# Weights rounded beside a spectrum: one piece begun at a time, and a later change of load buffers

## The chip, the cores and the metric

The kernel runs on one core of a Trainium2 chip. The metric is the time of one execution on the device in microseconds (us), the median of three runs. The engines are named as in the profile: PE is TensorE's matmul stream and PEld its weight loads, DVE is VectorE, ACT is ScalarE, POOL is GpSimd, SP is SyncE, whose queue (SPq) issues every transfer of this kernel.

## What is computed

Two batches of 3008 positions with 256 features pass a spectral layer and then two MLPs. The spectral layer takes a real FFT along the positions, mixes the features with a complex 256 x 256 matrix, adds a bias, pulls real and imaginary part towards zero by 0.01 and goes back:

```python
X = np.fft.rfft(x, axis=1)
Yr = Xr @ w_r - Xi @ w_i + b_r
Yi = Xr @ w_i + Xi @ w_r + b_i
Yr = np.sign(Yr) * np.maximum(np.abs(Yr) - 0.01, 0.0)
Yi = np.sign(Yi) * np.maximum(np.abs(Yi) - 0.01, 0.0)
y = np.fft.irfft(Yr + 1j * Yi, n=3008, axis=1)
h = y.reshape(6016, 256) @ w_in            # 256 x 2048
y = (h / (1 + np.exp(-h))) @ w_out         # 2048 x 256
h = y @ w_in2
out = np.maximum(0.01 * h, h) @ w_out2
```

All matmuls work on pairs of reduced-precision numbers: each float32 operand is split into a high and a low part (names ending in hi and lo, or h and l), and three products are summed. The weights are float64 in memory (two 32-bit words each) and have to be rounded to float32 on the chip before they are split.

## The kernel before

**Stages.** First comes a DFT over 47 points (L255, to about 47 us). Then 48 *items* (`items`, a frequency group k and a batch b) go through the spectrum. `spectrum(j)` (L366) runs eight stages, each on an item of another age (`STAGES`, L364): threshold (L334), split_a (L297), split_z (L316), split_y (L341) and store (L357) on ACT and DVE, then on PE mix (L307, tile pz), forward (L325, py) and backward (L349, pb). store copies pb to one of three buffers bo on ACT (L360) and sends it to memory, scr (L361). For the first 28 items one matrix dm serves two items; from item 28 on each item loads and splits its own (dmr, L213; dmh on ACT, L222; dml on POOL, L223). Then an inverse transform reads scr back (bt, L381; matmuls px, L408; splits xhi and xlo, L415 and L416), and the MLPs run over chunks of 512 positions, in steps f of 128 hidden features (ph, L505; acc, L575). The last items of the spectrum run between the first MLP steps.

**The weights beside it.** `weight_pieces` (L98) cuts w_in and w_out of the first MLP into 32 pieces of 128 x 256 numbers, 256 KB each; they are counted from 0 here. A piece passes five steps: `load` (L112) takes a buffer wraw and issues the transfer on SP; `begin` (L119) makes a rounded candidate on ACT (L123, L125) and DVE (L128, L130); `scale` (L133) reads wraw for the last time (DVE, L135); `around` (L139) adds on POOL (L142); `split` (L145) makes the two parts on ACT (L149) and POOL (L150). Each step hands the piece to the next by a list: loaded, begun, scaled, rounded, made.

Three drivers call them. `step` (L153) does a full round, during the DFT and in MLP steps f from 3 on (`between`). `third` (L169) is called after each item j of the loop at L386, with j % 3: at 0 it splits a piece and begins one, at 1 it scales the oldest begun piece, at 2 it adds and loads. `until` runs rounds until enough pieces are made.

**Buffers and order.** `raws` is a list of pools; `load` takes from the first. Up to item 32 that is the pool early with three buffers wraw, which lives in memory that the MLPs take over later; after `raws.pop(0)` it is the pool stage, with two (L115). Each engine works in the order in which the program names its instructions, and SP issues its transfers in that order too: a transfer whose buffer is still in use waits at the head of the queue.

Of the kernel before, what the change touches and what calls it, by code (L numbers as in the profile page):

```python
# [71 lines left out]
def spectral_mlp_kernel(ctx, tc, x, w_r, w_i, b_r, b_i, w_in1, w_out1, w_in2, w_out2, da, ea, dm, out):  # L72
# [23 lines left out]
    def weight_pieces(win, wout, in_dst, out_dst):  # L96

        win, wout = win.bitcast(U32), wout.bitcast(U32)
        pieces = []
        for q in range(NF // 2 + 1):
            if q < NF // 2:
                for d in range(2):
                    pieces.append((win[d * 128:(d + 1) * 128, q * 512:(q + 1) * 512], [w[:, d * DFF + q * 256:d * DFF + (q + 1) * 256] for w in in_dst]))
            if q:
                for f in (2 * q - 2, 2 * q - 1):
                    pieces.append((wout[f * 128:(f + 1) * 128, :], [w[:, f * D:(f + 1) * D] for w in out_dst]))
        loaded, begun, scaled, rounded, made = [], [], [], [], []  # L110

        def load():  # L112
            if pieces:
                src, dst = pieces.pop(0)
                raw = raws[0].tile([128, 512], F32, tag="wraw", name="wraw", bufs=3 if raws[1:] else 2).bitcast(U32)  # L115
                nc.sync.dma_start(out=raw, in_=src)
                loaded.append((raw.rearrange("p (e w) -> p e w", w=2), dst))

        def begin():  # L119
            raw, dst = loaded.pop(0)  # L120
            m = stage.tile([128, 256], U32, tag="wm", name="wm", bufs=2)
            c = stage.tile([128, 256], F32, tag="wc", name="wc", bufs=4).bitcast(U32)
            nc.scalar.activation(out=c, in_=raw[:, :, 0], func=ACTF.Copy, scale=2.0 ** -29)  # L123

            nc.scalar.activation(out=m.bitcast(F32), in_=raw[:, :, 1].bitcast(F32), func=ACTF.Copy, scale=2.0 ** -112)  # L125
            yield

            nc.vector.tensor_scalar(out=m.bitcast(F32), in0=m.bitcast(F32), scalar1=MAG, scalar2=-MAG, op0=ALU.min, op1=ALU.max)  # L128
            yield
            nc.vector.tensor_scalar(out=m, in0=m, scalar1=3, scalar2=0x7FFFFFFF, op0=ALU.logical_shift_left, op1=ALU.bitwise_and)  # L130
            begun.append((raw, m, c, dst))

        def scale():  # L133
            raw, m, c, dst = begun.pop(0)
            nc.vector.scalar_tensor_tensor(out=m, in0=raw[:, :, 1], scalar=0x80000000, in1=m, op0=ALU.bitwise_and, op1=ALU.bitwise_or)  # L135
            yield
            scaled.append((m, c, dst))

        def around(add):  # L139
            m, c, dst = scaled.pop(0)  # L140
            r = dst[0].bitcast(U32) if len(dst) == 1 else c
            add.tensor_tensor(out=r, in0=c, in1=m, op=ALU.add)  # L142
            rounded.append((c.bitcast(F32), dst))

        def split():  # L145
            c, dst = rounded.pop(0)
            if len(dst) == 2:
                hi, lo = dst
                nc.scalar.copy(hi, c)  # L149
                nc.gpsimd.tensor_tensor(out=lo, in0=c, in1=hi.bitcast(F32), op=ALU.subtract)  # L150
            made.append(1)

        def step(add=nc.gpsimd):  # L153

            if scaled:
                around(add)
            parts = [p() for p, ready in ((scale, begun), (begin, loaded and len(begun) < 2)) if ready]
            done = len(rounded)
            while parts:
                for p in list(parts):  # L160
                    if next(p, parts) is parts:
                        parts.remove(p)
            for _ in range(done):
                split()
            if scaled:
                around(add)
            load()

        def third(i):  # L169

            if i == 0:
                if rounded:
                    split()
                if loaded and len(begun) < 2:
                    list(begin())
            elif i == 1 and begun:
                list(scale())
            elif i == 2 and scaled:
                around(nc.gpsimd)
                load()  # L180

        def until(n):
            while len(made) < min(n, 2 * NF):
                step()

        return load, step, third, until

    raws, parts = [stage], ("hi", "lo")
# [177 lines left out]
    def spectrum(j):  # L366
        for part, lag in STAGES:
            if 0 <= j - lag < len(items):
                part(j - lag)
        split_dm(j + 1)  # L370
        load_dm(j + 4)
# [4 lines left out]
    def load_b():  # L376
        if groups:
            g, n = groups.pop(0)
            b, p = divmod(g, R2 // 2)
            bt = btp.tile([NJ, NG, D], F32, tag="bt", name="bt")  # L380
            nc.sync.dma_start(out=bt[:, :n], in_=scr[:, b, p:p + n, :])  # L381
            bts.append((g, n, bt))

    spectrum(-1)
    n_items = len(items)
    for j in range(n_items - 1):  # L386
        spectrum(j)
        if j == n_items - KH + KT + 6:
            load_b()
            load_b()  # L390
        if j == n_items - 16:
            raws.pop(0)
        third_w(j % 3)
    right.close()
# [370 lines left out]
```

## Time and profile before

| | |
|---|---|
| median of three runs | 1232.33 us |
| lowest, highest | 1231.36, 1234.48 us |
| profiled execution | 1230.04 us |
| its span, first to last instruction | 1228.3 us |
| PE busy in the span | 1201.3 us, 98% |
| DVE, ACT, POOL busy | 844.1, 782.0, 562.3 us |
| mean granted clock of PE | 0.996 |

The span leaves out what lies around the first and the last instruction, 1.7 us here. A busy PE is not PE at its peak, since its matmuls are pipelined; a share of busy time is an average over stages with different limits. So the profile is read stage by stage: stretches of the span with the busy time of each engine, then the timelines of the engines in the stretch where PE is not full, with the idle time before an instruction and what ended it, and the chain of waits. The granted clock is a share of 2.4 GHz; it has two levels, 1.0 and 0.5 (1.2 GHz), and a figure in between is a mean over a stretch. A release that the profile names can be wrong when an instruction waits for several things.

### The profile page before, as it was taken

To read this page: it belongs to the slowest core of one execution; us is meant where nothing else is said; L and a number is where in the kernel's file an instruction comes from. 1 tells how busy PE (TensorE), PEld (TensorE's weight loads), DVE (VectorE), ACT (ScalarE), POOL (GpSimd) and SP (SyncE) were. 2 spreads that over 40 slices of the span, in tenths; PEclk is the share of its full clock that TensorE was granted. 3 is DMA by queue.
4 is the path that set the end of the run, shared out by engine and by line. 5 is a ranking of instruction groups with operands and counts; after the bars stand their busy time and mean duration, and the time that the engine had idled before them with its cause. 6 is when DMAs were issued, how large, how long until landed. Compare 5 with 4: busy or idle time off the path is not lost.

```text
span 1228.3 us, 20097 instructions
## 1 busy us (share of the span) xinstructions
PE 1201.3 (98%) x7346; PEld 1074.2 (87%) x7346; DVE 844.1 (69%) x1533; ACT 782.0 (64%) x1614; POOL 562.3 (46%) x598
## 2 busy tenths in 40 slices
PE   8899978999999999999999999999999999999998
PEld 7788867888899999989998988988898898888898
DVE  2688855667888888888888896555555555555543
ACT  4788855566666666666666677566566566655664
POOL 0333522343445444544445484454545445554532
PEclk9999989999999999999999999999999999999999
DMA  9444443101011121111110100110111011001000
GB/s 233 126 119 126 123 124 90 39 14 48 18 54 50 40 70 48 43 41 61 38 27 26 35 31 1 35 35 1 35 36 35 1 35 35 10 26 35 31 1 31
DMA packets 35883, 61.62 MB, mean 50 GB/s; under 512 B 3908, under 2 KB 15784, under 8 KB 35784
## 3 DMA queue, kind: packets, MB, share of 16 engines
q1 hardware_dynamic: 35784, 60.33, 16.1%
q8 instruction: 58, 0.95, 0.3%
q14 instruction: 41, 0.34, 0.1%
HBM read 41.70 MB, written 18.61 MB: 49 GB/s over the span
## 4 chain that ended last, share of the span: by engine, by line
PE 91%; DMA 3%; DVE 3%; ACT 1%; issue 1%; SPq 0%; ACTq 0%; DVEq 0%
PE ph L505 42%; PE acc L575 38%; PE pz L312 5%; PE py L331 3%; PE px L408 2%; DMA wraw<-in_moe_w_in_dram 2%; PE pb L354 1%; DVE wlo L468 1%; DMA scr<-bo 1%; DMA xt<-in_x_dram 1%; PE pa L255 0%; SPq L237 0%; DVE py L339 0%; DVE lb L530 0%; DVE winlo L485 0%
## 5 line engine op out<-in xcount | busy, mean ns | idle before, releaser
L530 POOL TENSOR_TENSOR la<-u,ha 128x512 fp32r<-128x512 f32 (+1 forms) x176 | 232.6, 1322 | 246.8 <-ACT ha L568 246.0
L530 DVE TENSOR_TENSOR lb<-u,hb 128x768 fp32r<-128x768 f32 (+1 forms) x176 | 178.3, 1013 | 220.4 <-ACT hb L568 218.8
L505 PE MATMUL ph<-xlo,winhi 128*128 128x512 f32 (+1 forms) x768 | 239.2, 391 | 1.2 <-POOL xlo L431 1.2
L505 PE MATMUL ph<-xhi,winlo 128*128 128x512 f32 (+1 forms) x768 | 240.2, 394 | 0.1
L505 PE MATMUL ph<-xhi,winhi 128*128 128x512 f32 (+1 forms) x768 | 237.6, 391 | 0.0
L524 ACT ACTIVATE u<-ph 128x512 f32<-128x512 f32 (+1 forms) x192 | 113.7, 592 | 153.3 <-PE ph L505 153.2
L505 PEld LDWEIGHTS ph<-xlo,winhi 128*128 128x128 f32 x768 | 144.0, 188 | 36.3 <-POOL xlo L431 5.4
L505 PEld LDWEIGHTS ph<-xhi,winhi 128*128 128x128 f32 x768 | 143.8, 188 | 30.8
L542 POOL TENSOR_TENSOR u<-u 128x256 f32<-128x256 f32 x160 | 125.8, 786 | 65.1 <-DVE u L525 58.5
L568 ACT CAST hb<-u 128x768 fp32r<-128x768 f32 (+1 forms) x176 | 140.3, 797 | 9.4 <-DVE u L556 4.9
L575 PE MATMUL acc<-lb,whi 128*128 128x256 f32 (+1 forms) x496 | 141.1, 284 | 0.0
L575 PE MATMUL acc<-hb,whi 128*128 128x256 f32 (+1 forms) x496 | 139.6, 281 | 0.0
L575 PE MATMUL acc<-hb,wlo 128*128 128x256 f32 (+1 forms) x496 | 139.5, 281 | 0.0
L525 DVE SCALAR_TENSOR_TENSOR ph<-u,ph 128x512 f32<-128x512 f32 (+1 forms) x112 | 76.6, 684 | 77.8 <-ACT u L524 77.8
L527 ACT ACTIVATE ph<-ph 128x512 f32<-128x512 f32 (+1 forms) x96 | 55.1, 574 | 113.2 <-PE ph L505 113.2
L505 PEld LDWEIGHTS ph<-xhi,winlo 128*128 128x128 f32 x768 | 120.6, 189 | 2.8 <-ACT bo L360 0.3
L568 ACT CAST ha<-u 128x512 fp32r<-128x512 f32 (+1 forms) x176 | 109.7, 623 | 14.8 <-POOL u L542 14.8
L530 DVE TENSOR_TENSOR l<-ph,h 128x512 fp32r<-128x512 f32 (+1 forms) x176 | 117.4, 667 | 0.0
L549 DVE TENSOR_TENSOR u<-ph,u 128x512 f32<-128x512 f32 x160 | 109.3, 683 | 6.3 <-POOL u L542 6.3
L568 ACT CAST h<-ph 128x512 fp32r<-128x512 f32 (+1 forms) x176 | 102.3, 581 | 2.7 <-DVE ph L525 1.6
L575 PE MATMUL acc<-ha,whi 128*128 128x256 f32 (+1 forms) x352 | 102.1, 290 | 0.0
L575 PE MATMUL acc<-la,whi 128*128 128x256 f32 (+1 forms) x352 | 100.9, 287 | 0.0
(124 smaller groups left out, 2675.9 us busy)
## 6 DMA issues: line engine op xcount, KB each, us to landing
wraw<-in_moe_w_in_dram SPq DMA_DIRECT2D x32, 256.0 KB
wraw<-in_moe_w_out_dram SPq DMA_DIRECT2D x32, 256.0 KB
scr<-bo SPq DMA_DIRECT2D x48, 128.0 KB
scr<-x2o SPq DMA_DIRECT2D x22, 256.0 KB
x2i<-scr SPq DMA_DIRECT2D x22, 256.0 KB
out_dram<-x2o SPq DMA_DIRECT2D x22, 256.0 KB
dmr<-in_dm_dram SPq DMA_DIRECT2D x34, 160.0 KB
bt<-scr SPq DMA_DIRECT2D x14, 384.0 KB
```

The costliest lines, as they stand in the source:

```text
L312: nc.tensor.matmul(pz, lhsT=u[:, h, :], rhs=v[:, h].rearrange("p g e -> p (g e)"), start=(n == 0), stop=(n == len(terms) - 1))
L331: nc.tensor.matmul(py, lhsT=u, rhs=v, start=(n == 0), stop=(n == len(terms)))
L408: nc.tensor.matmul(px[:, s * PAIR:(s + 1) * PAIR], lhsT=bt[:, s, h * 128:(h + 1) * 128], rhs=ea_sb, start=True, stop=True, skip_group_chec ...
L505: nc.tensor.matmul(ph, lhsT=u[:, h, f * 128:(f + 1) * 128], rhs=v[:, h, :], start=(i == 0), stop=(i == len(terms) - 1))
L524: nc.scalar.activation(out=th, in_=ph, func=ACTF.Tanh)
L525: nc.vector.scalar_tensor_tensor(out=out, in0=th, scalar=1.0, in1=ph, op0=ALU.add, op1=ALU.mult)
L527: nc.scalar.activation(out=out, in_=ph, func=ACTF.Prelu, alpha=0.01)
L530: eng.tensor_tensor(out=lo, in0=src, in1=hi.bitcast(F32), op=ALU.subtract)
L542: nc.gpsimd.tensor_tensor(out=blk(1), in0=blk(0), in1=blk(2), op=ALU.subtract)
L549: nc.vector.tensor_tensor(out=v[:, 3:5], in0=b22, in1=v[:, 0:2], op=ALU.subtract)
L568: nc.scalar.copy(hi, src)
L575: nc.tensor.matmul(dst, lhsT=u, rhs=v, start=(begin and self.p == 0 and i == 0), stop=(end and self.p == NF // 2 - 1 and i == 2), skip_gro ...
```

## The change

```diff
--- before.py
+++ after.py
@@ -171,7 +171,7 @@
             if i == 0:
                 if rounded:
                     split()
-                if loaded and len(begun) < 2:
+                if loaded and not begun:
                     list(begin())
             elif i == 1 and begun:
                 list(scale())
@@ -388,7 +388,7 @@
         if j == n_items - KH + KT + 6:
             load_b()
             load_b()
-        if j == n_items - 16:
+        if j == n_items - 8:
             raws.pop(0)
         third_w(j % 3)
     right.close()
```

In `third`, a piece is begun only when no other piece has been begun and not scaled; before, a second one was let in. And the load that first takes a buffer of stage is that of item 41 (the first at or after item 40 with j % 3 == 2) and no longer that of item 32. The pools and their sizes are as they were.

What that does to the order of the instructions is shown at two places. The first is SP's queue at item 41, in one piece of the difference between the kernels: the load of piece 24 between the transfers of items 41 and 42 (wraw is the load's buffer, dmr the matrix, bo the item's result).

```order
 L361 DMA scr<-bo 4x32x256 [waits Activation_49]
 L213 DMA dmr<-in_dm_dram 128x320 [waits DMAHW7_49,DMAHW6_49,Pool_49]
-L116 DMA wraw<-in_moe_w_out_dram 128x512 [waits DVE_49]
+L116 DMA wraw<-in_moe_w_out_dram 128x512
 L361 DMA scr<-bo 4x32x256 [waits DMAHW0_49,Activation_49]
 L213 DMA dmr<-in_dm_dram 128x320 [waits DMAHW2_49,DMAHW1_49,Pool_49]
```

The rows stand where they stood; the wait for DVE is gone from this row, and in the same way from that of piece 25, three items later. The row of piece 23, at item 38, reads the same in both kernels, with a wait for DVE; but it waited for the scale step of piece 21 and now waits for that of piece 20. The loads of pieces 21 and 22, which waited for no engine, now wait for the scale steps of 18 and 19.

The second place is DVE at the first two rounds in the MLP (f = 3 and 4). In the kernel before, with wraw_2320 the buffer of piece 24 and wraw_2463 that of piece 25 (wm is the candidate; L525 and L530 belong to the MLP):

```order
L135 SCALAR_TENSOR_TENSOR wm_2508<-wraw_2320,wm_2508 128x256
L128 TENSOR_SCALAR wm_2750<-wm_2750 128x256
L130 TENSOR_SCALAR wm_2750<-wm_2750 128x256
L530 TENSOR_TENSOR la_2723<-ph_2715,ha_2722 128x512
L530 TENSOR_TENSOR lb_2725<-ph_2736,hb_2724 128x512
L525 SCALAR_TENSOR_TENSOR ph_2779<-u_2790,ph_2779 128x512
L135 SCALAR_TENSOR_TENSOR wm_2750<-wraw_2463,wm_2750 128x256
```

In the changed kernel wraw_2314 is the buffer of piece 24:

```order
L128 TENSOR_SCALAR wm_2743<-wm_2743 128x256
L130 TENSOR_SCALAR wm_2743<-wm_2743 128x256
L530 TENSOR_TENSOR la_2717<-ph_2709,ha_2716 128x512
L530 TENSOR_TENSOR lb_2719<-ph_2730,hb_2718 128x512
L525 SCALAR_TENSOR_TENSOR ph_2771<-u_2782,ph_2771 128x512
L135 SCALAR_TENSOR_TENSOR wm_2743<-wraw_2314,wm_2743 128x256
```

The first round scaled piece 24 and began 25; now it begins 24, and the scale step of 24 follows in the second round, behind the MLP's L530 and L525. The load of piece 26, which takes the buffer of 24, is issued in the first round in both kernels. All later rounds of this kind are shifted in the same way, and one more round has work to do.

## Rows read from the trace of the kernel before

**Rows 1.** Stretches: length, busy time (x instructions) of each engine, PEclk, DMA share, GB/s
```profile
47.00:131.00 84.00, 83.93 (x511) 74.83 (x512) 73.42 (x161) 73.86 (x209) 32.11 (x40) 1.00 0.37 110
...
139.63:147.82 8.19, 8.06 (x50) 6.79 (x49) 7.05 (x16) 7.33 (x22) 4.21 (x6) 1.00 0.47 140
147.82:158.62 10.80, 9.88 (x58) 8.01 (x56) 7.99 (x17) 7.48 (x22) 4.77 (x6) 1.00 0.34 99
158.62:169.82 11.20, 8.56 (x48) 6.77 (x48) 7.02 (x15) 7.50 (x21) 4.20 (x5) 1.00 0.33 102
169.82:174.28 4.46, 1.46 (x10) 1.28 (x11) 2.57 (x7) 3.89 (x11) 1.68 (x3) 0.74 0.55 186
174.28:182.40 8.12, 8.12 (x32) 7.54 (x33) 3.45 (x7) 2.44 (x6) 1.47 (x2) 0.51 0.39 117
182.40:197.50 15.10, 10.58 (x60) 8.59 (x59) 7.06 (x14) 7.19 (x18) 0.00 (x0) 1.00 0.20 60
197.50:660.00 462.50, 462.50 (x2782) 409.63 (x2781) 381.72 (x689) 293.38 (x578) 211.75 (x238) 1.00 0.14 45
```

**Rows 2.** Timeline of the SP queue, 147 to 204 us: start, length, line, transfer
```profile
147.52 0.34 SPq L213 DMA_DIRECT2D dmr<-in_dm_dram  x1
153.38 0.33 SPq L116 DMA_DIRECT2D wraw<-in_moe_w_in_dram  x1
153.82 0.54 SPq L361 DMA_DIRECT2D scr<-bo  x1
...
164.18 0.33 SPq L116 DMA_DIRECT2D wraw<-in_moe_w_out_dram  x1
...
169.74 0.82 SPq L381 DMA_DIRECT2D bt<-scr  x2
175.34 0.35 SPq L116 DMA_DIRECT2D wraw<-in_moe_w_out_dram  x1
...
199.39 4.65 SPq L116 DMA_DIRECT2D wraw<-in_moe_w_in_dram  x2
```

**Rows 3.** Timeline of DVE, 152 to 180 us, same columns, [idle before <-releaser]
```profile
152.25 1.10 DVE L135 SCALAR_TENSOR_TENSOR wm<-wraw,wm 128x256 uint32<-128x256 uint32 x1
...
174.23 1.08 DVE L135 SCALAR_TENSOR_TENSOR wm<-wraw,wm 128x256 uint32<-128x256 uint32 x1
...
179.98 0.41 DVE L346 TENSOR_TENSOR yl<-py,yh 128x256 fp32r<-128x256 f32 x1
```

**Rows 4.** Timeline of ACT, 158 to 178 us, same columns as rows 3
```profile
158.62 0.37 ACT L360 COPY bo<-pb 128x256 f32<-128x256 f32 x1 [2.46 <-DMA scr<-bo]
...
164.80 0.38 ACT L360 COPY bo<-pb 128x256 f32<-128x256 f32 x1
...
169.82 0.37 ACT L360 COPY bo<-pb 128x256 f32<-128x256 f32 x1 [2.86 <-DMA scr<-bo]
...
173.36 0.38 ACT L360 COPY bo<-pb 128x256 f32<-128x256 f32 x1
...
178.02 0.47 ACT L415 CAST xhi<-px 128x376 fp32r<-128x376 f32 x1 [1.23 <-PE px L408]
```

**Rows 5.** Chain of waits, 147 to 202 us: start, length, engine and line
```profile
147.90 0.36 PE pb L354 x3
148.26 1.40 PE pz L312 x6
149.65 0.83 PE py L331 x7
...
174.28 3.70 PE px L408 x16
...
201.87 0.87 PE px L408 x8
```

**Rows 6.** One stretch of the tail of the spectrum, same columns as rows 1
```profile
187.85:193.90 6.05, 2.02 (x9) 1.40 (x9) 2.61 (x6) 2.47 (x8) 0.00 (x0) 1.00 0.09 28
```

**Rows 7.** Timeline of ACT in the MLP's first chunk, same columns as rows 3
```profile
203.11 0.43 ACT L123 ACTIVATE wc<-wraw 128x256 uint32<-128x256 uint32 x1 [0.55 <-DMA wraw<-in_moe_w_in_dram]
```

## The prediction

> **What bounds the kernel now.** I read the stretches first [rows 1]. From 197.50 us to 660 TensorE (PE) is busy for all of its time, and so it is from 47 to 131 (83.93 of 84 us). Nothing that the change moves on other engines in those two stretches can shorten or, while PE stays fed, lengthen the run; what can be won lies between. There the spectrum runs in groups of three items, and the stretches are cut where the ACT copy of bo (L360) begins that stands just ahead of each begin step. An undisturbed group takes 8.19 us (139.63 to 147.82). The next two take 10.80 and 11.20 us, and then PE works at half of its clock, 0.51, for 8.12 us.
>
> The second view is the queue of SyncE (SP), which issues every transfer [rows 2]. After 147.52 it stands still until 153.38, then issues one weight load (L116), and everything behind that load comes out in a bunch: stores of bo, then dmr. It stands again until 164.18, and until 175.34. What it waits for is on VectorE (DVE) [rows 3]: the scale step L135 begins at 152.25 and takes 1.10 us, so it ends at 153.35, and the load goes out 0.03 later; the third begins at 174.23, ends at 175.31, and the load goes at 175.34. These are loads 23, 24 and 25 (counted from 0), the third to fifth that go to the common pool, where wraw has two buffers. Three pieces are in flight there, so load 23 wants the buffer of piece 21, whose scale step comes two items later in the program than the load.
>
> The third view is what stands behind it [rows 4]. bo has three buffers. ACT's copy at 158.62 had stood 2.46 us for a store that had not landed, the one at 169.82 2.86 us. PE needs what these copies free, and runs dry. So the bound here is the SP queue, held up by a weight load that nobody needs yet.
>
> **The change, part by part.** *Loads change over 8 items from the end.* Loads 21, 22 and 23 now go to the early pool of three buffers, where each finds a buffer whose scale step ended one item before; 24 and 25 are the first users of the two common buffers and wait for no engine. All three stalls in the loop go. What is late next is the ordinary three-item pattern of ACT and DVE, 8.19 us a group:
> - group of load 23: 10.80 - 8.19 = 2.61 us
> - group of load 24: 11.20 - 8.19 = 3.01 us
>
> Behind load 24, the first inverse product (px, L408) begins at 174.28 [rows 5]. The page blames ACT, but the copy that frees its buffer begins at 173.36 and ends at 173.74 [rows 4]; what px also needs is bt, issued at 169.74 [rows 2], so bt took at most 4.54 us. In the changed kernel the copy that now begins at 164.80 [rows 4] begins 2.61 earlier, at 162.19; its store goes at about 162.6 and bt at some 163.2; with 4.54 us it lands by 167.8. px then waits only for its copy, at 173.74 - 5.62 = 168.12. That takes away 174.28 - 173.74 = **0.54 us**, with 0.3 us in hand. Load 25 follows bt and no longer holds back the stores.
>
> *The clock.* The granted clock of 169.82 to 174.28 is 0.74 on average, and 0.51 up to 182.40 [rows 1]: it fell to the 1.2 GHz level about (1 - 0.74) x 4.46 / 0.5 = 2.3 us ahead of 174.28, at 172, and came back at 182. Ahead of the fall PE had been busy 8.56 of 11.20 us, then 1.46 of 4.46. In the changed kernel those gaps go. PE's item that starts its pz at 148.26 is through at 148.26 + 1.40 + 0.83 + 0.36 = 150.85 [rows 5]; the one ahead of px stands two groups later, so it ends at 167.2, and px starts at 168.1: a gap of about 1 us. I take the clock as staying at 1.0. Of the tail that remains one stretch, 187.85 to 193.90, has PE busy 2.02 of 6.05 us with the clock at 1.00 [rows 6]. The Trainium skill has a rule that speaks against this term (TensorE: Matmul & The Clock Gate, "A second HAM failure mode: psum-queue depth-cycling"): short idles between groups of matmuls, if frequent enough, make the clock go down and up. By it the tail could bring the clock down again, and the sum would be 6.16 instead of 8.94; the trace agrees with it at 172 and not in the tail. What is the term worth? From 174.28 to 182.40 PE ran 16 px, one pz, one py and one pb. At full clock these take 2 x 0.87 + 1.40 + 0.83 + 0.36 = 4.33 us [rows 5], so at most 8.12 - 4.33 = 3.79. But py takes a buffer of the tag h that yl (L346) releases, and yl ends at 180.39 [rows 3], 2.37 us after the second xhi copy of ACT begins at 178.02 [rows 4]. With px done 1.74 us after its start, xhi begins 1.78 after it, yl ends at 4.15, and py and pb add 1.19: 5.34 instead of 8.12. I take **2.78 us**, with the ends 0 (the clock falls all the same) and 3.79 (that chain is no limit).
>
> *One piece begun at a time.* At item 0 two ACT and two DVE steps go (L123, L125, L128, L130); one set comes back in the first MLP chunk, a step later. PE is full from 47 to 131 and after 197.5 [rows 1], so that is worth nothing; without that cover it would be about two ACT instructions like the 0.43 us one of [rows 7], 0.9 us. In between each scale step follows its own begin by one item instead of four; the engines' order and the number of steps are otherwise as before.
>
> *Where the wait goes.* At the loop's end two pieces are loaded and none is begun. In the MLP steps load 26 is therefore issued ahead of the scale step that frees its buffer, and stands at the head of SP's queue for one step. Behind it stand only loads 27 to 31 and bt loads; all stores of bo are ahead of it. A load and its begin step both move one step later, so the time between them stays. The first such load went at 199.39 [rows 2] and ACT took it at 203.11 after 0.55 us of waiting [rows 7], with PE full all the while. Cost: nothing.
>
> **Sum.** 2.61 + 3.01 + 0.54 + 2.78 = 8.94 us. The profiled execution took 1230.04 us (span 1228.3 and 1.74 around it), so it would take 1221.1. The median of the runs shown, 1232.33, lies 2.29 above it, and I put the forecast on the median: 1232.33 - 8.94 = **1223.4 us**.
>
> **The rivals.**
> - *The clock falls anyway.* The queue is freed, but the tail of the spectrum still has its gaps [rows 6], and the clock goes down in one of them for as long as it did. Against it: it did not there, and the gaps ahead of 172 are the ones that go. Then the 2.78 is lost: 1232.33 - 6.16 = 1226.2. Chance 0.2.
> - *The queue is free and nothing is won.* If the stores are slow by themselves, bo's buffers come free as late as now. The store that held the copy at 169.82 [rows 4] went out behind load 24, after 164.18 + 0.33 [rows 2], so it took at most 5.3 us, in a bunch; three buffers at a third of 8.19 us an item cover 8.19, which speaks against it. It would give 1232 (1229 to 1233). Chance 0.09.
> - *Slower.* The wait taken into the MLP's first chunk turns into a wait of ACT: load 26 and its successors land after ACT reaches their begin step, and the casts for PE (L535) stand behind it. If each of six loads (26 to 31) were exposed for its whole flight, 203.11 - 199.39 = 3.72 us, that is 22.3 us: 1223.4 + 22.3 = 1245.7. It decides from 8.94 / 6 = 1.5 us a step on PE. Against it: load and begin step move together, and PE has waited for nothing there. Chance 0.03.
>
> **How the numbers follow.** The forecast's own case has 0.68. Within 0.3% (3.7 us) is about what a measurement of this kernel can tell from no change. The forecast and the clock rival both lie beyond it on the fast side: 0.68 + 0.2 = 0.88, less 0.01 for a median that lands close: faster 0.87, same 0.10, slower 0.03. The range goes from 1220.1 (all of the clock's 3.79 won, 9.95 in all, from the profiled execution's 1230.04) to 1228.0 (the clock rival, 1226.2, and 1.8 for the spread of the runs and a bt that lands late). It leaves out the two last rivals and a little more.
>
> **What would show it.** SP issues load 23 within about half a us of the dmr ahead of it, and 24 and 25 likewise; the copies of bo wait for no store; the two groups after 147.82 take about 8.2 us each; px begins at about 168.2; the granted clock stays at 1.0 from 168 to 180; PE is full from about 189 instead of 197.5. In the first MLP chunk SP stands for loads 26 to 31 up to one step each, and PE does not. I am wrong in the size if the clock shows 0.5 again; wrong in the mechanism if copies of bo still wait for stores though the loads do not stand; and wrong in sign if PE has waits between 190 and 225.

## The result and the profile after

The changed kernel takes 1220.51 us (median of six runs, 1219.68 to 1221.55), beside 1231.84 us of the kernel before in the same session (1229.54 to 1235.85): a ratio of 0.9905 (it comes from all the runs, so it is not the quotient of the two medians), 95% interval 0.9886 to 0.9925, and 11.3 us faster by the medians. Run again in two other sessions (e7 and e10 below), it gave ratios of 0.9920 and 0.9928, 9.9 and 8.6 us by the medians. The forecast was 8.94 us, that is 1223.4 us with a range from 1220.1 to 1228.0: the time lies in the range, 0.4 us from its fast end. The profiled execution took 1220.56 us, with a span of 1218.8 us (before: 1228.3).

The stretches of the changed kernel are cut at the same copies of bo as [rows 1], and the columns are those of [rows 1]. Only the last cut differs: 197.50 lies at the first acc (L575) of the kernel before, 186.85 lies 1.23 us ahead of that of the changed one.

```profile
47.00:131.00 84.00, 84.00 (x516) 75.08 (x516) 73.15 (x160) 73.69 (x208) 33.37 (x41) 1.00 0.37 110
...
146.78:154.99 8.21, 8.06 (x50) 6.80 (x49) 7.07 (x16) 7.36 (x23) 4.21 (x6) 1.00 0.48 142
154.99:163.19 8.20, 8.05 (x50) 6.78 (x49) 7.06 (x16) 7.33 (x22) 4.21 (x6) 1.00 0.46 142
163.19:167.17 3.98, 3.02 (x20) 2.55 (x18) 3.02 (x7) 3.58 (x12) 2.13 (x3) 1.00 0.77 234
167.17:171.65 4.48, 4.48 (x33) 4.21 (x34) 3.95 (x8) 2.75 (x7) 1.59 (x2) 1.00 0.46 150
171.65:186.85 15.20, 10.69 (x55) 8.71 (x54) 6.36 (x13) 6.64 (x17) 0.00 (x0) 0.89 0.21 63
186.85:660.00 473.15, 473.15 (x2848) 419.12 (x2848) 391.00 (x706) 300.98 (x592) 216.28 (x243) 1.00 0.14 44
```

The groups of loads 23 and 24 took 10.80 and 11.20 us and now take 8.21 and 8.20. The stretch from the last of these copies to the first px has shrunk from 4.46 to 3.98 us, the one from px to the second px from 8.12 to 4.48, and its clock is 1.00. The tail behind it shows something new, a mean clock of 0.89: from the second px to the first acc it takes 16.43 us, where it took 15.11.

The SP queue, beside [rows 2], shows why:

```profile
146.47 0.33 SPq L213 DMA_DIRECT2D dmr<-in_dm_dram  x1
146.86 0.66 SPq L116 DMA_DIRECT2D wraw<-in_moe_w_in_dram  x1
...
154.67 0.33 SPq L213 DMA_DIRECT2D dmr<-in_dm_dram  x1
155.05 0.42 SPq L116 DMA_DIRECT2D wraw<-in_moe_w_out_dram  x1
...
162.19 0.88 SPq L381 DMA_DIRECT2D bt<-scr  x2
163.12 0.42 SPq L116 DMA_DIRECT2D wraw<-in_moe_w_out_dram  x1
```

Each of loads 23, 24 and 25 goes out right behind the transfer ahead of it, where 23 and 24 had stood until 153.38 and 164.18 and 25 until 175.34. The first bt, at 169.74 before, now goes at 162.19.

On ACT no copy of bo waits for a store any more, so the rows that answer to [rows 4] carry no bracket:

```profile
154.99 0.41 ACT L360 COPY bo<-pb 128x256 f32<-128x256 f32 x1
...
163.19 0.42 ACT L360 COPY bo<-pb 128x256 f32<-128x256 f32 x1
166.74 0.38 ACT L360 COPY bo<-pb 128x256 f32<-128x256 f32 x1
```

And PE, beside [rows 5]:

```profile
167.17 2.02 PE L408 MATMUL px<-ea_sb,bt 96*128 96x94 f32 x16 [0.96 <-ACT bo L360]
...
170.46 0.28 PE L331 MATMUL py<-bias,pick 128*128 128x256 f32 x1
...
171.65 1.03 PE L408 MATMUL px<-ea_sb,bt 96*128 96x94 f32 x8
...
183.15 0.58 PE L354 MATMUL pb<-yh,dml 128*128 128x256 f32 x1 [2.43 <-ACT bo L360]
...
188.08 0.40 PE L575 MATMUL acc<-ha,woutlo 128*128 128x512 f32 x1
```

px begins 0.05 us after the copy of 166.74 has ended (0.38 us later): it waits for its copy alone and no longer for bt. (The landing events in the traces agree: the first bt was there at 166.96, 0.16 us ahead of the copy's end; in the kernel before it came at 174.19, 0.09 us ahead of px.) The pb at 183.15 takes 0.58 us. In the kernel before, the same pb, behind the same wait, took 0.39:

```profile
193.90 0.39 PE L354 MATMUL pb<-yh,dml 128*128 128x256 f32 x1 [2.43 <-ACT bo L360]
```

The clock of the changed kernel in steps of 2 us says why:

```profile
182.00:184.00 2.00, 0.85 (x4) 0.85 (x5) 1.22 (x4) 1.55 (x4) 0.00 (x0) 0.67 0.00 0
184.00:186.00 2.00, 2.00 (x6) 1.61 (x6) 0.91 (x2) 0.08 (x1) 0.00 (x0) 0.50 0.27 73
186.00:188.00 2.00, 2.00 (x11) 1.64 (x10) 0.69 (x1) 0.86 (x2) 0.00 (x0) 0.97 0.00 1
```

By these means the granted clock went down to the 1.2 GHz level at about 182.7, inside the wait of 2.43 us, and was back at about 186.1.

**Where 9.43 us came from.** Each line is a difference of two lags, that is of how far the changed kernel is ahead at two marks. The marks of before stand in [rows 1], [rows 4] and [rows 5], but for two: its first pz (L312) began at 47.07 and its first acc (L575) at 197.51.

| from mark to mark | before | after | ahead by | won |
|---|---|---|---|---|
| start to first pz | 47.07 | 46.44 | 0.63 | 0.63 |
| to the copy of bo ahead of load 23 | 147.82 | 146.78 | 1.04 | 0.41 |
| to the copy two groups later | 169.82 | 163.19 | 6.63 | 5.59 |
| to px | 174.28 | 167.17 | 7.11 | 0.48 |
| to the second px | 182.40 | 171.65 | 10.75 | 3.64 |
| to the first acc | 197.51 | 188.08 | 9.43 | -1.32 |

From the first acc to the end of the span it is 1030.79 us before and 1030.72 after: the whole MLP stage is the same to 0.1 us.

### The profile page after: what moved, and what is told of

The parts are those of the page before. It is cut to its first block, busy times and chain, and to the rows that moved or that the text cites. A ratio compares the mean times of both kernels' runs of the same rounds, so it can differ in the third digit from the quotient of the medians.

```text
span 1218.8 us, 20110 instructions
## 1 busy us (share of the span) xinstructions
PE 1200.3 (98%) x7346; PEld 1075.3 (88%) x7346; DVE 843.8 (69%) x1533; ACT 782.3 (64%) x1614; POOL 562.9 (46%) x598
## 4 chain that ended last, share of the span: by engine, by line
PE 94%; DMA 2%; DVE 2%; ACT 1%; POOL 1%; issue 1%; SPq 0%; ACTq 0%; DVEq 0%; POOLq 0%
PE ph L505 42%; PE acc L575 38%; PE pz L312 5%; PE py L331 3%; PE px L408 2%; PE pa L255 1%; PE pb L354 1%; DMA xt<-in_x_dram 1%; DMA wraw<-in_moe_w_out_dram 1%; DVE wlo L468 0%; PE warm L246 0%; POOL xlo L431 0%; DVE py L339 0%; ACT bo L360 0%; POOL la L530 0%
## 5 line engine op out<-in xcount | busy, mean ns | idle before, releaser
L530 POOL TENSOR_TENSOR la<-u,ha 128x512 fp32r<-128x512 f32 (+1 forms) x176 | 232.7, 1322 | 246.8 <-ACT ha L568 246.0
L530 DVE TENSOR_TENSOR lb<-u,hb 128x768 fp32r<-128x768 f32 (+1 forms) x176 | 178.1, 1012 | 220.7 <-ACT hb L568 219.0
L575 PE MATMUL acc<-lb,whi 128*128 128x256 f32 (+1 forms) x496 | 141.1, 284 | 0.0
L575 PE MATMUL acc<-hb,whi 128*128 128x256 f32 (+1 forms) x496 | 139.6, 281 | 0.0
L575 PE MATMUL acc<-hb,wlo 128*128 128x256 f32 (+1 forms) x496 | 139.5, 281 | 0.0
L525 DVE SCALAR_TENSOR_TENSOR ph<-u,ph 128x512 f32<-128x512 f32 (+1 forms) x112 | 76.6, 684 | 78.8 <-ACT u L524 78.8
L530 DVE TENSOR_TENSOR l<-ph,h 128x512 fp32r<-128x512 f32 (+1 forms) x176 | 117.2, 666 | 0.0
L575 PE MATMUL acc<-ha,whi 128*128 128x256 f32 (+1 forms) x352 | 102.1, 290 | 0.0
L575 PE MATMUL acc<-la,whi 128*128 128x256 f32 (+1 forms) x352 | 100.9, 287 | 0.0
```

The costliest lines, as they stand in the source:

```text
L525: nc.vector.scalar_tensor_tensor(out=out, in0=th, scalar=1.0, in1=ph, op0=ALU.add, op1=ALU.mult)
L530: eng.tensor_tensor(out=lo, in0=src, in1=hi.bitcast(F32), op=ALU.subtract)
L575: nc.tensor.matmul(dst, lhsT=u, rhs=v, start=(begin and self.p == 0 and i == 0), stop=(end and self.p == NF // 2 - 1 and i == 2), skip_gro ...
```

## The experiments

All ratios are to the kernel before on the same chip, each from 5 to 12 executions of the kernel that is tried. Two figures of their profiles are compared: the first pz, which ends the DFT stage, and the time from it to the first acc, which holds the spectrum (150.44 us before, 141.64 after).

**e1: the pop alone.**

```diff
-        if j == n_items - 16:
+        if j == n_items - 8:
```

> Only the later change of pool; two pieces may be begun, as before. Theory (the head of SP's queue, held by loads 23 to 25): the whole gain is here, 0.989 to 0.993 of the time before, some 1221 us; SP issues loads 23, 24 and 25 within 0.7 us of the dmr or bt ahead of them, no copy of bo waits for a store, px begins near 167.5. Rival (the begin rule carries the gain, by taking work from ACT and DVE): about 1231, ratio 0.998 to 1.001.

Measured: 1222.28 us beside 1231.38, ratio 0.9929 (0.9914 to 0.9944). First pz to first acc: 140.82. The queue and PE of e1:

```profile
148.88 0.49 SPq L116 DMA_DIRECT2D wraw<-in_moe_w_in_dram  x1
157.07 0.43 SPq L116 DMA_DIRECT2D wraw<-in_moe_w_out_dram  x1
164.20 0.88 SPq L381 DMA_DIRECT2D bt<-scr  x2
```

```profile
169.31:173.75 4.44, 4.44 (x33) 4.18 (x33) 3.82 (x8) 2.62 (x7) 1.59 (x2) 1.00 0.47 151
173.75:188.84 15.09, 10.58 (x61) 8.59 (x60) 7.06 (x14) 7.19 (x18) 0.00 (x0) 1.00 0.22 63
```

Loads 23 and 24 go out 8.2 us apart as in the changed kernel (25, at 165.13, behind bt), px to second px (the first of the two stretches) takes 4.44 us, and here the clock stayed at 1.00 in the tail as well: 15.09 us against 15.10 in [rows 1]. px begins at 169.31 and not near 167.5, since in this execution the first pz came at 48.02. The pop by itself brings the gain, as far as these runs can tell: 9.1 us by the medians, beside 8.6 to 11.3 for the whole change.

**e2: the begin rule alone.**

```diff
-                if loaded and len(begun) < 2:
+                if loaded and not begun:
```

> Only one piece begun at a time; the pool changes at item 32 as before. Theory: loads 23 to 25 stand at the head of SP's queue as before, groups of 10.8 and 11.2 us after the first of 8.2, px near 174, ratio 0.998 to 1.001; at most 0.4 us earlier from the begin step that item 0 no longer has. Rival (the begin rule carries the gain): 0.990 to 0.995.

Measured: 1231.73 us beside 1231.38, ratio 0.9995 (0.9983 to 1.0007). All three loads still stand (until 158.50, 169.57 and 180.53 in an execution whose first pz came at 49.93), and copies of bo wait as in [rows 4]:

```profile
164.00 0.37 ACT L360 COPY bo<-pb 128x256 f32<-128x256 f32 x1 [2.77 <-DMA scr<-bo]
...
174.98 0.37 ACT L360 COPY bo<-pb 128x256 f32<-128x256 f32 x1 [2.67 <-DMA scr<-bo]
```

With the late pop alone making 9.1 us and the rule alone none, the rule is not what frees the queue.

**e3: six buffers bo, nothing else.** The loads stand as before; only the copies get more room.

```diff
-        bo = f3.tile([128, D], F32, tag="bo", name="bo")
+        bo = f3.tile([128, D], F32, tag="bo", name="bo", bufs=6)
```

> The kernel before with six buffers bo instead of three; loads 23 to 25 still stand in SP's queue. Theory: the stall reaches PE by two ways, the copies of bo (2.61 and 3.01 us) and bt behind load 24. The first goes, so both groups take 8.2 us; the second stays: load 24 goes near 161.5, bt near 167, px near 171.5 instead of 174.3, and the clock still falls, so 2.8 us faster, some 1229, ratio 0.997 to 0.999. Rival 1 (bo is the only way): 0.990 to 0.993. Rival 2 (late stores do no harm, the groups are long for another reason): groups of 10.8 and 11.2 us, ratio 1.000.

Measured: 1230.48 us beside 1231.38, ratio 0.9997 (0.9985 to 1.0009): a miss. No copy waits for a store now, but the groups behind loads 23 and 24 are still long, since ACT now stops right behind the copy, at the cast of dmr:

```profile
158.62 0.46 ACT L222 CAST dmh<-dmr 128x320 fp32r<-128x320 f32 x1 [2.58 <-DMA dmr<-in_dm_dram]
...
169.52 0.46 ACT L222 CAST dmh<-dmr 128x320 fp32r<-128x320 f32 x1 [2.63 <-DMA dmr<-in_dm_dram]
```

The chain of waits of e3 (start, length, what) names the same two loads:

```profile
154.07 4.53 DMA dmr<-in_dm_dram
...
164.88 4.61 DMA dmr<-in_dm_dram
...
173.83 3.70 PE px L408 x16
```

The matrix dmr, too, was queued behind the standing load and came out in the bunch; its split is the next thing that ACT and PE need. The waits of 2.58 and 2.63 us stand where 2.46 and 2.86 stood for the stores [rows 4]. The stores are not the only way by which the standing load reaches PE.

**e4: the pop three items later than before**, so that load 23 is free and 24 and 25 stand.

```diff
-        if j == n_items - 16:
+        if j == n_items - 13:
```

> The kernel before with the change of pool at item 35 instead of 32, so that only loads 24 and 25 stand. Theory: the group behind load 23 takes 8.2 us instead of 10.8, the one behind load 24 still 11.2, px and the clock as before but 2.6 us earlier: some 1229.2, ratio 0.997 to 0.999. Rival (one stall is as bad as two, since bt and the clock take what is left): ratio 0.9995 to 1.001, or all gained: 0.990 to 0.993.

Measured: 1229.82 us beside 1231.38, ratio 0.9987 (0.9975 to 0.9999), 1.6 us faster. One group is back at its pattern, 149.18 to 157.37 (8.19 us), the other is not:

```profile
149.18 0.41 ACT L360 COPY bo<-pb 128x256 f32<-128x256 f32 x1
...
157.37 0.41 ACT L360 COPY bo<-pb 128x256 f32<-128x256 f32 x1
...
168.42 0.37 ACT L360 COPY bo<-pb 128x256 f32<-128x256 f32 x1 [2.71 <-DMA scr<-bo]
```

```profile
172.90:181.14 8.24, 8.24 (x32) 7.66 (x33) 3.44 (x7) 2.44 (x6) 1.46 (x2) 0.50 0.40 116
```

From its first pz to its first acc it took 147.97 us, 2.47 less than before: one standing load, one group. The clock (last row) still fell ahead of px, so the clock term comes with the last group, not with the first.

**e5: load 25 alone stands** (`n_items - 10`).

> The kernel before with the pop at n_items - 10: loads 23 and 24 are the first users of the two common buffers, and load 25 alone still stands for a scale step, behind the two bt loads. Theory: a standing load costs time only through the stores of bo and the loads of dmr and bt queued behind it, and behind load 25 there are only stores that nobody waits for soon. Then this kernel is as fast as the pop alone: ratio 0.990 to 0.995 to the kernel before, load 25 issued some 5 us late, no copy of bo waiting for a store, px of 16 about 2 us long with the granted clock at 1.00. Rival (each standing load costs some 3 us by itself): ratio 0.995 to 0.997. That load 25's stand brings the clock down at px would show as px of 3.7 us and a ratio near 0.996.

Measured: 1223.98 us beside 1232.12, ratio 0.9932 (0.9914 to 0.9950); first pz to first acc 142.37. SP and PE:

```profile
163.79 0.89 SPq L381 DMA_DIRECT2D bt<-scr  x2
170.34 0.35 SPq L116 DMA_DIRECT2D wraw<-in_moe_w_out_dram  x1
```

```profile
168.79 2.02 PE L408 MATMUL px<-ea_sb,bt 96*128 96x94 f32 x16 [0.99 <-ACT bo L360]
```

The stretch from px to the second px:

```profile
168.79:174.80 6.01, 6.01 (x32) 5.50 (x33) 3.95 (x8) 2.75 (x7) 1.60 (x2) 0.72 0.40 116
```

Load 25 stands 5.7 us behind bt and delays neither a copy of bo nor px: where a load stands decides, not that it stands. One part of the expectation failed: in this execution the clock went down at about 171 and came back at about 174.4, although PE had idled only 0.99 us ahead of px. That made px to second px 6.01 us instead of 4.44 (e1), some 1.6 us.

**e6: the loads stand, both ways to PE covered.** Five buffers bo, five buffers dmr, each dmr loaded two items earlier.

```diff
-            dm_raw[j] = dmp.tile([128, 320], F32, tag="dmr", name="dmr", bufs=3)
+            dm_raw[j] = dmp.tile([128, 320], F32, tag="dmr", name="dmr", bufs=5)
...
-        bo = f3.tile([128, D], F32, tag="bo", name="bo")
+        bo = f3.tile([128, D], F32, tag="bo", name="bo", bufs=5)
...
-        load_dm(j + 4)
+        load_dm(j + 6)
...
+    load_dm(4)
```

> The kernel before with its three standing loads left in, but with five buffers bo and with dmr loaded two items earlier into five buffers (both held three). Theory: the stand reaches PE by two ways only, the stores (bo) and dmr; with both covered the groups of loads 23 and 24 take 8.2 us each although the loads still stand, and bt, issued behind load 24's stand, is late next: px waits 2 us or more for it, and the clock falls there. Expected ratio 0.994 to 0.998 (5.6 us of the groups gone, of which bt takes back some 2 to 3 us, clock not won). Rival (the groups are long for another reason than these two, for instance the DMA engines themselves): groups stay near 11 us and the ratio is 0.999 to 1.001.

Measured: 1226.57 us beside 1232.12, ratio 0.9957 (0.9942 to 0.9973). The copies that bound the two groups, with loads 23 and 24 issued only at 154.35 and 162.56:

```profile
148.78 0.41 ACT L360 COPY bo<-pb 128x256 f32<-128x256 f32 x1
...
157.00 0.41 ACT L360 COPY bo<-pb 128x256 f32<-128x256 f32 x1
...
165.21 0.41 ACT L360 COPY bo<-pb 128x256 f32<-128x256 f32 x1
```

```profile
167.08 0.81 SPq L381 DMA_DIRECT2D bt<-scr  x2
```

```profile
165.21:171.88 6.67, 3.00 (x20) 2.56 (x19) 4.55 (x9) 3.88 (x12) 3.70 (x5) 1.00 0.46 149
171.88:179.47 7.59, 7.59 (x33) 7.01 (x33) 2.42 (x5) 2.44 (x6) 0.00 (x0) 0.55 0.42 128
```

Both groups take 8.2 us although the loads stand: apart from the stores and dmr nothing had made them long. That dmr is a way of its own e3 shows; that the stores are one is read from the waits of [rows 4], and covering dmr alone was not run. bt, issued at 167.08 and in e1 at 164.20, with the same copy beginning at 165.21 and 165.20, is late next: px begins at 171.88 instead of 169.31 (e1), 2.74 us behind the end of its copy (168.76 + 0.38). Behind that gap the clock falls and px to second px takes 7.59 us instead of 4.44. First pz to first acc is 146.62 against 140.82 in e1: 5.8 us, of which the later px makes 2.57 and the stretch with the clock down 3.15.

**e7: the changed kernel again, beside e5 and e6.**

> The changed kernel once more, beside the kernel before and the kernel with the pop at n_items - 10 on the same chip. Theory: the begin rule by itself is worth nothing or up to 0.5 us, so the ratio is 0.990 to 0.994 and within 0.15% of the late-one kernel's. Rival (the begin rule frees ACT early in the spectrum and so gains 1 to 2 us once the loads no longer stand): ratio lower than the late-one kernel's by 0.001 to 0.002. The granted clock is 1.00 around px; a short fall behind it, near 183 us, may come in one profiled execution and not in the other.

Measured: 1222.18 us beside 1232.12, ratio 0.9920 (0.9901 to 0.9939); px to second px 4.45 us, clock 1.00 there, and a fall again in the tail, from about 185 to 188. First pz to first acc is 141.86. It is 1.8 us ahead of e5 by the medians, and the intervals overlap; e5's own fall at px makes such a difference by itself. So the begin rule's worth isn't told apart from nothing here.

**e8, e9: fewer pieces in the DFT stage.** The changed kernel with the rounding beside the DFT begun three (e8) or five (e9) steps later; that many pieces move into the MLP. e8:

```diff
-            if c in (1, 2):
+            if c in (4, 5):
...
-            elif 2 < c < 12:
+            elif 5 < c < 12:
```

e9 has `c in (6, 7)` and `7 < c < 12`.

> The changed kernel with the weight rounding of the DFT stage begun three steps later (first loads at c = 4 and 5, rounds from c = 6), so that three pieces fewer are loaded and worked on while the DFT goes on and three more rounds fall into the MLP. Theory (the DFT stage, where PE isn't full, is set by transfers and ACT): 0.77 MB fewer to move there, the first pz 1 to 3 us earlier, ratio to the kernel before 0.987 to 0.991, 1 to 3 us faster than the changed kernel. Rival (the DFT stage is set by its own loads and by PE's clock): first pz within 0.5 us, ratio as the changed kernel's. Rival on the other side: the three further rounds in the MLP make PE wait for pieces, which shows as PE waits behind 200 us and a ratio above the changed kernel's.

> The changed kernel with the weight rounding of the DFT stage begun five steps later (first loads at c = 6 and 7, rounds from c = 8): five pieces fewer there, five more rounds in the MLP. Theory (each piece left out of the DFT stage gives back about half a us: the first pz came at 46.03 with three pieces fewer, against 46.44 and 47.66 in two profiles of the changed kernel): first pz at 45 to 46, ratio to the changed kernel's 0.997 to 0.999. Rival (three pieces were already all that the stage could give back, or the first pz of 46.03 was scatter): same as e8 or as the changed kernel within 0.1%. On the other side: the first MLP chunk runs short of pieces, PE waits behind 200 us, ratio above the changed kernel's.

Measured: e8 1220.61 us (1216.95 to 1222.47) beside 1232.12, ratio 0.9900 (0.9879 to 0.9920), first pz at 46.03. e9 1224.15 us (1221.59 to 1227.11) beside 1232.51, ratio 0.9933 (0.9912 to 0.9953): its first pz came at 43.84, the earliest of all, and what that won is lost in the first MLP chunk. PE's waits in e9, from 200 to 330 us (line waited for; total, times, longest):

```profile
PE acc L575 <- POOL woutlo L150: 3.5, 2, 2.4
PE ph L505 <- POOL winlo L150: 2.0, 1, 2.0
```

From its first acc to the end of the span it took 1037.68 us, 6.96 more than the changed kernel; these two waits are 5.5 of it. In all it ends where the changed kernel did beside it (e10 below, 1223.89 us). The rival on the other side that e9's expectation named is what happened: the first MLP chunk runs short of pieces.

**e10, e11: the changed kernel and e8 once more, side by side.**

> The changed kernel, beside the two with a later start of the weight rounding. Theory: ratio 0.990 to 0.993 to the kernel before; first pz between 46.4 and 47.7; granted clock 1.00 at px, with a short fall somewhere behind 180 us in the profile or none.

> The changed kernel with the weight rounding begun three steps later, as in e8, once more beside the changed kernel. Theory: first pz about 46.0, ratio 0.9985 to the changed kernel's. Rival: no difference (within 0.05%), so that the 1.6 us of e8 was scatter.

Measured beside 1232.51 us: e10 1223.89 (1220.71 to 1227.72), ratio 0.9928 (0.9907 to 0.9949), first pz at 49.56; e11 1219.30 (1218.70 to 1220.28), ratio 0.9894 (0.9875 to 0.9914), first pz at 44.17. All five runs of e11 lie below all six of e10. With e8 and e7 the same way round, 1.6 us apart (their runs overlap), three pieces fewer in the DFT stage make a version that beats the changed kernel. By how much is open: the two pairs say 1.6 and 4.6 us, and the first pz scatters. In ten profiles with the DFT stage as it was it came between 46.44 and 49.93, the latest in two (e2 and e10) whose clock was down when the spectrum began.

## Why the prediction was right, step by step

- **The stalls.** Predicted to go for 2.61 + 3.01 = 5.62 us; 5.59 went. e1, e4 and e6 say why from three sides: without the stands the groups are 8.2 us, with one stand taken away one group is, and with the stands left in but stores and dmr covered both are. The prediction's picture had one hole: it named the stores (bo) as the way from SP to PE, and the dmr that comes out in the same bunch only in passing. e3 shows that dmr alone keeps the groups long. The size came out right all the same, since the change frees both.
- **bt.** Predicted 0.54 us and px at 168.12; it was 0.48 and 167.17, the rest being the 1.04 us by which everything came earlier. px waits for its copy alone, and load 25, behind bt, holds nothing that is needed (e5).
- **The clock.** Predicted 2.78 us between 0 and 3.79; from px to the second px it was 3.64. The step that failed is "py takes a buffer of the tag h that yl (L346) releases". In the changed kernel py began at 170.46, directly behind pz, ahead of the yl that answers to the one in [rows 3]:

```profile
171.20 0.41 DVE L346 TENSOR_TENSOR yl<-py,yh 128x256 fp32r<-128x256 f32 x1
```

So py did not wait for that yl. In the kernel before, py began at 180.39, just as yl ended, but it began directly behind pz there too, at half clock: two things that fell on one moment were read as cause and effect. At full clock the stretch is nearly PE's work alone, 4.48 us against the 4.33 worked out from single products.
- **The clock rival** had a chance of 0.2 and was priced as the loss of the whole clock term. It came true in another place and smaller: in the tail behind px, in this execution, for 1.32 us. The prediction had named a clock of 0.5 as the sign that its size is wrong, and by that sign this term was. The waits there (1.61 and 2.43 us of pb for ACT) are the same in all these kernels, and the clock fell in them or just behind in the profiles of the changed kernel, e7, e8 and e11, not in e1, e5, e9 and e10 (of the kernels with the longer gap at px, it fell there in e2 and e3 too). The section of the Trainium skill that the prediction weighed (TensorE: Matmul & The Clock Gate, "A second HAM failure mode: psum-queue depth-cycling") says that short idles between groups of matmuls, if frequent enough, make the clock go down and up. The traces agree with it in the tail of four of these eight executions, and no run here shows what decides in which.
- **The begin rule.** Predicted worth nothing where PE is full. From the first pz to the copy of bo 76.2 us later both kernels agree to 0.01 us: 47.07 to 123.26 before, 46.44 to 122.64 after. Then one group differs. The copies of bo on ACT before:

```profile
123.26 0.41 ACT L360 COPY bo<-pb 128x256 f32<-128x256 f32 x1
...
131.44 0.41 ACT L360 COPY bo<-pb 128x256 f32<-128x256 f32 x1
```

After:

```profile
122.64 0.41 ACT L360 COPY bo<-pb 128x256 f32<-128x256 f32 x1
...
130.35 0.44 ACT L360 COPY bo<-pb 128x256 f32<-128x256 f32 x1
```

That is 8.18 us against 7.71; 0.41 of the difference is left at the mark of the table. So the rule may be worth 0.4 us where nothing was forecast: the four profiles with the rule and the DFT stage as it was (after, e2, e7, e10) all have the short group. But it isn't simply the rule's: of the six with the old rule e3 has the short group (123.29 to 130.99), and e8, with the new rule and the later rounding, has the long one (122.22 to 130.40), as have e9 and e11. What decides it is open.
- **The MLP.** Predicted: loads 26 to 31 stand for up to a step, at no cost. ACT's wait for the piece, 0.55 us in [rows 7], is longer, but from the first acc to the end nothing changed (1030.79 and 1030.72 us). So the slower rival's mechanism is there in small, covered by PE's full work; in e9, with five pieces fewer in hand, PE does wait. The row of ACT:

```profile
196.87 0.44 ACT L123 ACTIVATE wc<-wraw 128x256 uint32<-128x256 uint32 x1 [1.50 <-DMA wraw<-in_moe_w_in_dram]
```

- **The size.** The forecast put 8.94 us on the median. The terms measured 5.59 + 0.48 + 3.64 - 1.32 = 8.39 us in the profiles. That this lies so near to the forecast is in part luck: the clock at px gave 0.86 us more than its term, and the tail took 1.32 us back. The rest of the 9.43 is the earlier start of the spectrum (0.63), which scatters from execution to execution by more than that, and the one short group (0.41). The 11.3 us of the first comparison are its high end; 9.9 and 8.6 followed.

## What to carry to other kernels

A transfer that waits for a buffer holds up everything behind it on its queue, so price a prefetch by what is queued behind it, follow each of these to the engine that wants it (here stores, matrices and the next stage's input, of which covering one only uncovered the next), and check that its buffer comes free before its turn. Work moved out of one crowded stage pays until the stage that takes it runs out of stock: three pieces moved were a gain, and five gave it back. Two events that end at the same moment in one trace need not be cause and effect; a second trace at another clock or with another order tells. And where a short gap may or may not bring the clock down, take the price from rows and expect it in some executions only.

## What the runs showed of the chip that was not expected

- The clock does not follow the size of a single gap alone. In the five kernels with a gap of 2.58 us or more ahead of px it fell there (px took 3.70 us in four and 3.07 in e6), but at different places: some 0.3 us into the gap in the kernel before, 3.9 us into it in e3, 0.7 us behind it in e6. In the eight with about 1 us it stayed in seven, and in e5 it fell for some 3.4 us all the same. In or just behind the same two waits of 1.61 and 2.43 us in the tail it fell in four of these eight executions. In the DFT stage, from 8 us on, it fell in every profile but those of the kernel before and of e7, at places between 23 and 45 us.
- Transfers that came out in a bunch behind a standing one also took longer from issue to landing. By the landing events in the trace of the kernel before, the dmr issued from 120 to 148 us landed 2.4 to 4.1 us after their issue, and the five that came out behind loads 23 and 24 took 4.5 to 6.5 us. In e3 the two of its chain took 4.53 and 4.61 us.
